# Linear attention gated by an FFN: rest stacks in buffers of their own and at other steps, bias copies at other steps, a rest matmul at four places

## The chip, the cores and the metric

One core of a Trainium2 chip runs the whole kernel. The metric is the device time of one execution in microseconds (us). Several executions are timed and the median is given. One execution is recorded by the hardware profiler; all times inside the kernel are from it, counted from the first instruction.

The core has five engines. TensorE multiplies matrices (PE; PEld is its load of the stationary operand), VectorE (DVE), ScalarE (ACT) and GpSimd (POOL) work on tiles in the on-chip memory, and SyncE (SP) issues most DMA transfers. Each engine works through its own instructions in order.

## What is computed

```python
def reference(x, wqkv, wo, w1, b1, w2, b2):          # x: 1 x 2048 x 576, F = 4608
    xn = layernorm(x)
    q, k, v = split(xn @ wqkv)                       # 32 heads of 18
    pq, pk = phi(q), phi(k)                          # phi(t) = where(t > 0, t + 1, exp(t)) + 1e-6
    kv, z = einsum(pk, v), sum(pk)                   # one state per head, no softmax
    s = (pq @ kv / (pq @ z + 1e-6)) @ wo
    g = silu(gelu(xn @ w1 + b1) @ w2 + b2)
    return x + s * g
```

Everything is float32. There are two halves, a linear attention and an FFN of width 4608, and the FFN's silu gates the attention's output.

## The kernel before

Every product is computed from a high and a low part of each operand: a cast on ScalarE makes the high part (hi), a subtraction on VectorE the low part (lo), and three matmuls (high by high, high by low, low by high) stand for one. The large products are also split into blocks and computed with seven block products in place of eight, which needs sums of blocks of both operands, made once and kept in DRAM where they are used more than once.

The program has three stages.

*Pairs 0 to 7* (to 155 us). A pair is two row tiles of 128 tokens. They are normalized and transposed, keys and values are computed, and the attention state is summed up. In the gaps the block sums of w2 are made (`w2_hi`, `w2_lo`, lines 565 to 577) and stored.

*Pairs 8 to 15 and a last half* (155 to 308 us). Queries are computed, wo is folded into the state, and the attention's output is written per row tile to s_dram. The denominators are made by `den_mul` on GpSimd (line 926).

*The FFN* (308 to 1082 us, then a tail). Tokens are taken in two halves, and for each half F in nine chunks (18 in all, `HOps`). A chunk has two block pairs (`Up`, numbered by `self.p`); for each, `Up.mm` (line 1280 on) makes the seven block products of x by w1 in PSUM, ScalarE applies the gelu, and the down products `pm` (line 1430) are added up in the tile `macc` by VectorE. `macc` starts from the bias b2: `load_bias` (line 1262) brings two rows of it by DMA into two blocks of `macc`, and four calls of `set_bias` (line 1267) copy them on ScalarE to all places. At the half switch the old `macc` is combined and stored to `c_dram` first.

D is 576, that is four blocks of 128 and a rest of 64. The rest's rows (of x and of w1) are handled by `Rest` (line 314): for each of seven stacks it loads a tile of 128 x 512 (`rs`), casts it (`hi`, line 326, ScalarE) and subtracts (`lo`, line 330, VectorE) in two groups of 3 and 4 blocks, `sums` in between (lines 347 and 349, four small instructions), and stores the results (line 341) to `we_dram` or `xe_dram` with SyncE. In the FFN each product has seven matmuls, six for the blocks and one for the rest: `we` by `x_extra` or a piece of x.

What sets the order. The work around the pairs is listed in `plans`, a table from a step number to calls. A pair has 14 steps (`NSP`), step = pair x 14 + position, and at each step the calls filed under it are issued. For the rest stacks `REST_PLAN` (line 792) gives (pair, position) of the load, the first group's lo, the sums and the second group's lo; hi comes a step before lo and the store a step after. A chunk of the FFN has 28 steps (`NS`) in the same table. VectorE, ScalarE, GpSimd and TensorE follow the program's order. SyncE issues its transfers in an order of its own, one after the other, and each waits until an earlier one, mostly the one eight before it, has landed. The stacks' tiles `re` have the tag "stw" of the pool `w1r`, two buffers, which `w2_hi` and other stagings use as well.

Of the kernel before, what the change touches and what calls it, by code (L numbers as in the profile page):

```python
# [9 lines left out]
F32R = mybir.dt.float32r  # L10
# [5 lines left out]
P = 128  # L16
# [23 lines left out]
NSP = 14  # L40
# [5 lines left out]
def linear_attention_gated_ffn(ctx, tc, x, wqkv, wo, w1, w1e, b1, w2, b2, out):  # L46
    nc = tc.nc
# [267 lines left out]
    class Rest:  # L315
# [6 lines left out]
        def hi(self, g):  # L322
            n = (3, 4)[g]
            t = w1r.tile([P, 2, 4, P], F32R, tag="stw", name=f"re{self.i}{self.of_x}{g}")
            self.t[g] = t = t[:, :, :n]
            nc.scalar.copy(t[:, 0], self.s[:, :n])
# [348 lines left out]
    def k_sum(k):  # L675
# [5 lines left out]
    W2_SPLITS = (  # L681
        (2, 4, 6), (2, 9, 12), (3, 4, 6), (3, 9, 12), (4, 4, 6), (4, 9, 12), (5, 7, 9), (6, 7, 9), (7, 1, 3),
    )
# [3 lines left out]
    def plan_pair(p):  # L687
# [102 lines left out]

    rests = {}
    REST_PLAN = {
        (0, True): ((2, 12), (3, 2), (3, 4, GP), (4, 2)),
        (0, False): ((4, 0), (5, 2), (5, 13, DV), (6, 2)),
        (1, False): ((4, 7), (5, 2), (5, 13, DV), (6, 2)),
        (2, False): ((8, 9), (9, 12), (9, 12, DV), (10, 6)),
        (3, False): ((9, 9), (10, 6), (10, 11, DV), (11, 6)),
        (4, False): ((11, 1), (12, 6), (12, 9, DV), (13, 6)),
        (1, True): ((13, 1), (14, 6), (14, 9, DV), (15, 6)),
    }  # L800

    def plan_rests():
        for key, (load, first, (p, k, eng), second) in REST_PLAN.items():
            add(load[0] * NSP + load[1], lambda key=key: rests.update({key: Rest(*key)}))
            for g, (q, at) in enumerate((first, second)):
                step = q * NSP + at
                add(step - 1, lambda key=key, g=g: rests[key].hi(g))
                add(step, lambda key=key, g=g: rests[key].lo(g))
                add(step + (2 if step == 9 * NSP + 12 else 1), lambda key=key, g=g: rests[key].store(g))
            add(p * NSP + k, lambda key=key, eng=eng: rests[key].sums(eng))  # L810

# [57 lines left out]
    kwp = ph2.enter_context(tc.tile_pool(name="kwp", bufs=1, reuse_waits="tile"))  # L869
    t2 = ph2.enter_context(tc.tile_pool(name="t2", bufs=2, side="right", reuse_waits="tile"))  # L870
    wo_sb = []
    for i, (g, n) in enumerate(GROUPS):
# [234 lines left out]
    EL1 = nc.vector  # L1107
    kept = []
    w1t, w2_raw0 = {}, []

# [150 lines left out]

    def load_bias():
        for h, m in enumerate(BIAS):
            src = bass.AP(tensor=b2.tensor, offset=b2.offset + h * HD, ap=[[0, P], [1, HD]])
            nc.sync.dma_start(macc[:, 0, m, :], src)

# [6 lines left out]
    class Up:  # L1273
# [10 lines left out]
        def mm(self, ps, i, first=True):  # L1284
            (wh, wl), (h, l) = self.w.product(i), self.xb[i]
            seq = []
            for k in range(2):
                seq += [(wh[:, k], h[:, k]), (wh[:, k], l[:, k]), (wl[:, k], h[:, k])]
            seq += [(self.w.rest(i), xrest[i])]
            for n, (st, mv) in enumerate(seq):  # L1290
                nc.tensor.matmul(  # L1291
                    ps.rearrange("p (c j) -> p c j", c=4), st, mv, start=first and n == 0, stop=n == len(seq) - 1,
                    skip_group_check=True,
                )
# [329 lines left out]
    n_chunks = 2 * NC  # L1624
    load_bias()
    for step in range(n_chunks):
# [4 lines left out]
        if c == 0:  # L1631
            if half:
                add(base + 8, load_bias)
            for at, m in zip((12, 13, 15, 17), (C11, C22, C21, C12)):
                add(base + at, set_bias, m)
# [148 lines left out]
```

## Time and profile before

| what | us |
|---|---|
| three runs, median (lowest to highest) | 1141.03 (1137.71 to 1145.02) |
| the profiled execution, its time | 1137.64 |
| the profiled execution, its span from first to last instruction | 1135.9 |
| TensorE busy in the span | 1102.8 (97%) |
| mean clock granted to TensorE | 0.986 of full speed |
| VectorE, ScalarE, GpSimd busy | 826.5, 515.7, 452.5 |

The timeline of an engine lists its instructions with the start, the duration, the line, the output and inputs, and in brackets how long the engine was idle before it and who ended that ("<-DVE k L422": VectorE's instruction of line 422 that writes k). Instructions on an engine overlap a little, so a duration can reach into the next start. The windows view gives for a stretch A:B its length, then the busy time and count of instructions on each engine, then the granted TensorE clock, the DMA engines' busy share and GB/s. In the chain of waits each row is a start, a duration and what the end of the kernel hung on then; "DMA a<-b" is the time from a transfer's issue to its landing.

### The profile page before, as it was taken

The page shows a single profiled execution, that of the slowest core. Times are in us where ns is not written, and L with a number is a line of the kernel's source. Part 1 is how long each engine was busy: PE and PEld are TensorE (multiplying, and loading weights), DVE is VectorE, ACT ScalarE, POOL GpSimd, SP SyncE. Part 2 cuts the span into 40 slices and gives each one's busy share as a digit, 9 for nine tenths or more (in the row PEclk, how much of TensorE's full clock was granted, in tenths as well). Part 3 has the DMA queues.
Part 4 walks back from the last instruction along what each step waited for, and adds up shares of the span by engine and source line. Part 5 has one row for each costly group of instructions (what it writes and reads, how often), then busy time and mean ns, then how long its engine had stood idle before and what let it go on. Part 6 is the DMA issues. An engine that isn't in the chain of part 4 may idle for free.

```text
span 1135.9 us, 18977 instructions
## 1 busy us (share of the span) xinstructions
PE 1102.8 (97%) x6888; PEld 1018.9 (90%) x6888; DVE 826.5 (73%) x1284; ACT 515.7 (45%) x945; POOL 452.5 (40%) x421
## 2 busy tenths in 40 slices
PE   8999998999999999999999999979999999999998
PEld 8999997999989989989889899878998988989988
DVE  6776857888588878888888788655674664755766
ACT  7765645554564444554544444433242242342342
POOL 6844153454552543544534524313232242341310
PEclk9999898999999999999999999989999999999999
DMA  5989856896998796796887969987667667777343
GB/s 203 322 281 346 306 177 195 293 349 229 331 376 292 249 358 202 274 341 215 309 293 231 349 195 358 386 310 254 201 231 232 217 219 226 220 223 230 96 147 119
DMA packets 116059, 295.02 MB, mean 260 GB/s; under 512 B 12221, under 2 KB 31677, under 8 KB 113919
## 3 DMA queue, kind: packets, MB, share of 16 engines
q1 hardware_dynamic: 110495, 282.61, 70.3%
q0 software_dynamic: 4896, 10.03, 5.4%
q8 instruction: 54, 0.88, 0.3%
q10 hardware_dynamic: 576, 1.18, 0.3%
q14 instruction: 38, 0.31, 0.1%
HBM read 180.39 MB, written 108.66 MB: 254 GB/s over the span
## 4 chain that ended last, share of the span: by engine, by line
PE 79%; DMA 7%; DVE 6%; ACT 3%; issue 3%; POOL 1%; SPq 1%; DVEq 0%; POOLq 0%; ACTq 0%
PE pm L1430 33%; PE zy L1291 10%; PE a L1291 9%; PE e L1291 9%; PE b L1291 5%; PE ps_s L989 4%; PE pd L1545 2%; PE e L414 1%; PE pl L470 1%; PE z L414 1%; DMA wa<-op_a 1%; DMA rs2False<-w1e 1%; PE a L414 1%; DMA op<-w2o 1%; DMA op<-w 1%
## 5 line engine op out<-in xcount | busy, mean ns | idle before, releaser
L1019 ACT CAST h_h<-g 128x512 fp32r<-128x512 f32 x204 | 120.2, 621 | 137.8 <-PE pm L1430 136.6
L1022 DVE TENSOR_TENSOR h_l<-g,h_h 128x512 fp32r<-128x512 f32 x204 | 161.5, 792 | 8.9 <-ACT h_h L1019 8.9
L1438 DVE TENSOR_TENSOR macc<-macc,pm 128x576 f32<-128x576 f32 x136 | 102.1, 751 | 40.1 <-PE pm L1430 40.1
L1291 PE MATMUL a<-xH,wa 128*128 128x512 f32 x288 | 101.4, 393 | 0.0
L1440 DVE TENSOR_TENSOR macc<-pm,macc 128x576 f32<-128x576 f32 x98 | 74.2, 757 | 24.9 <-PE pm L1430 23.5
L1398 POOL TENSOR_TENSOR mid<-g 128x512 f32<-128x512 f32 x34 | 44.5, 1309 | 105.2 <-ACT g L1299 105.2
L1299 ACT ACTIVATE g<-b,b1c 128x512 f32<-128x512 f32 x36 | 24.8, 688 | 134.6 <-DVE b L1317 134.6
L1291 PEld LDWEIGHTS a<-xH,wa 128*128 128x128 f32 x288 | 54.0, 188 | 11.3
L1308 ACT COPY mid<-a 128x512 f32<-128x512 f32 x36 | 21.2, 588 | 94.7 <-PE a L1291 94.7
L1392 POOL TENSOR_TENSOR g<-g 128x512 f32<-128x512 f32 x34 | 49.9, 1468 | 25.8 <-DVE h_l L1022 24.4
L1311 DVE TENSOR_TENSOR mid<-b,mid 128x512 f32<-128x512 f32 x36 | 24.7, 685 | 44.8 <-PE b L1291 42.8
L1395 POOL TENSOR_TENSOR g<-g 128x512 f32<-128x512 f32 x34 | 51.3, 1508 | 12.5 <-DVE h_l L1022 10.4
L1291 PE MATMUL a<-xL,wa 128*128 128x512 f32 x144 | 56.2, 390 | 0.0
L1516 POOL TENSOR_TENSOR fin1l<-fin1h,fin1l 128x288 f32<-128x288 f32 x8 | 6.5, 807 | 120.4 <-DVE macc L1438 42.6
L1291 PE MATMUL e<-xSH,wb 128*128 128x512 f32 x144 | 50.5, 391 | 1.3 <-DVE b L1317 1.1
L1291 PE MATMUL zy<-xSH,w 128*128 128x512 f32 x144 | 50.9, 394 | 0.0
L1291 PE MATMUL zy<-xH,w 128*128 128x512 f32 x144 | 50.9, 394 | 0.0
L1291 PE MATMUL b<-xSH,w 128*128 128x512 f32 x144 | 50.5, 391 | 0.0
L1291 PE MATMUL e<-xSH,w 128*128 128x512 f32 x144 | 50.4, 390 | 0.0
L1389 POOL TENSOR_TENSOR g<-g 128x512 f32<-128x512 f32 x34 | 47.1, 1385 | 2.7
L1046 POOL TENSOR_TENSOR mid<-w1raw 128x256 f32<-128x256 f32 x17 | 13.3, 782 | 84.7 <-DMA w1raw<-w 57.3
L676 POOL TENSOR_TENSOR zacc<-zacc,k 128x576 f32<-128x576 f32 x16 | 25.6, 1602 | 53.2 <-ACT k L507 52.6
(965 smaller groups left out, 3711.3 us busy)
## 6 DMA issues: line engine op xcount, KB each, us to landing
op<-w SPq DMA_DIRECT2D x72, 256.0 KB
w<-op SPq DMA_DIRECT2D x72, 256.0 KB
we<-we_dram SPq DMA_DIRECT2D x36, 448.0 KB
w2raw<-w SPq DMA_DIRECT2D x10, 1152.0 KB
op<-w2o SPq DMA_DIRECT2D x19, 576.0 KB
w1raw<-w SPq DMA_DIRECT2D x18, 512.0 KB
op_a<-wa SPq DMA_DIRECT2D x18, 512.0 KB
wa<-op_a SPq DMA_DIRECT2D x18, 512.0 KB
```

Source lines behind the costliest of these rows:

```text
L414: nc.tensor.matmul(ps, st, mv, start=first and n == 0, stop=n == len(seq) - 1, skip_group_check=True,)
L989: nc.tensor.matmul(self.ps[h], st[:, k, :], w[:, k, h * HD : (h + 1) * HD], start=(i == 0), stop=(i == len(self.seq) - 1),)
L1019: nc.scalar.copy(pair[0], src)
L1022: eng.tensor_tensor(pair[1], src, pair[0].bitcast(F32), op=SUB)
L1291: nc.tensor.matmul(ps.rearrange("p (c j) -> p c j", c=4), st, mv, start=first and n == 0, stop=n == len(seq) - 1, skip_group_check=True,)
L1389: tt(src[5, pr], A(1, 1), A(1, 0), op=SUB)
L1392: tt(src[6, pr], src[5, pr], A(0, 0), op=ADD)
L1395: tt(src[3, pr], src[6, pr], A(0, 1), op=SUB)
L1398: tt(src[7, pr], A(0, 0), A(1, 0), op=SUB)
L1430: nc.tensor.matmul(ps[:, q, :HD], hs[p][st][:, cs], m[:, p, :], start=(n == 0 and i not in CHAIN), stop=(n == len(seq) - 1), skip_group_ch ...
L1438: nc.vector.tensor_tensor(dst, dst, src, op=SUB)
L1440: nc.vector.tensor_tensor(dst, src, dst, op=ADD)
```

## The change

It has four parts.

*Rest stacks.* The tiles `re` get a pool and tag of their own: in the pairs the pool `t1` with one buffer, from pair 8 on the pool `t2` with two. `REST_PLAN` has new steps for loads, groups and sums; at most one of the early stacks is in work in a pair. Stack (2, False) is loaded in the set-up of the second stage. The sums of five stacks stand at position 6 or earlier of a pair (two of them behind position 9 to 13 before). The sums of (0, True) stay on GpSimd, a pair later; the others stay on VectorE. The split of w2's sum 6 in pair 5 moves three positions earlier.

*Half 0's bias.* Its load is unchanged; the four copies move from steps 12, 13, 15 and 17 of the first chunk to 5, 6, 7 and 8, the second and third in swapped order.

*Half 1's bias.* Its load moves from step 8 of the chunk on SyncE's queue to step 5 on GpSimd's; the copies move to steps 10, 11, 13 and 14.

*The rest matmul.* In `Up.mm` it was the last of the seven of a product. It is now the seventh, first, fourth or sixth for block pairs 0, 1, 2 and 3 (by `self.p % 4`).

```diff
--- before.py
+++ after.py
@@ -321,7 +321,8 @@
 
         def hi(self, g):
             n = (3, 4)[g]
-            t = w1r.tile([P, 2, 4, P], F32R, tag="stw", name=f"re{self.i}{self.of_x}{g}")
+            pool, bufs = rest_pool
+            t = pool.tile([P, 2, 4, P], F32R, tag="re", name=f"re{self.i}{self.of_x}{g}", bufs=bufs)
             self.t[g] = t = t[:, :, :n]
             nc.scalar.copy(t[:, 0], self.s[:, :n])
 
@@ -679,7 +680,7 @@
 
     K_UP = (1, 6, 7, 5, 2, 4, 3)
     W2_SPLITS = (
-        (2, 4, 6), (2, 9, 12), (3, 4, 6), (3, 9, 12), (4, 4, 6), (4, 9, 12), (5, 7, 9), (6, 7, 9), (7, 1, 3),
+        (2, 4, 6), (2, 9, 12), (3, 4, 6), (3, 9, 12), (4, 4, 6), (4, 9, 12), (5, 4, 6), (6, 7, 9), (7, 1, 3),
     )
     W2_STARTS = ((1, 7), (2, 2), (2, 11), (3, 2), (3, 11), (4, 2), (4, 11), (6, 0), (6, 8))
     W2_LOADS = {1: (13, 1), 3: (7, 2), 5: (7, 3)}
@@ -788,26 +789,30 @@
         if p == 6:
             add(base + 12, lambda: wkq.sums(cur["rq"][0], GP))
 
-    rests = {}
+    rests, rest_pool = {}, (t1, 1)
     REST_PLAN = {
-        (0, True): ((2, 12), (3, 2), (3, 4, GP), (4, 2)),
-        (0, False): ((4, 0), (5, 2), (5, 13, DV), (6, 2)),
-        (1, False): ((4, 7), (5, 2), (5, 13, DV), (6, 2)),
-        (2, False): ((8, 9), (9, 12), (9, 12, DV), (10, 6)),
-        (3, False): ((9, 9), (10, 6), (10, 11, DV), (11, 6)),
-        (4, False): ((11, 1), (12, 6), (12, 9, DV), (13, 6)),
-        (1, True): ((13, 1), (14, 6), (14, 9, DV), (15, 6)),
+        (0, True): ((3, 0), (4, 2), (4, 4), (5, 2)),
+        (0, False): ((4, 7), (5, 13), (6, 2), (6, 4)),
+        (1, False): ((5, 7), (6, 12), (6, 13), (7, 4)),
+        (2, False): (None, (9, 12), (10, 6), (10, 11)),
+        (3, False): ((10, 12), (11, 6), (12, 6), (13, 6)),
+        (4, False): ((12, 12), (13, 6), (14, 6), (15, 6)),
+        (1, True): ((14, 12), (15, 6), (16, 1), (16, 3)),
     }
 
+    def load_rows(key):
+        rests[key] = Rest(*key)
+
     def plan_rests():
-        for key, (load, first, (p, k, eng), second) in REST_PLAN.items():
-            add(load[0] * NSP + load[1], lambda key=key: rests.update({key: Rest(*key)}))
+        for key, (load, first, sums, second) in REST_PLAN.items():
+            if load:
+                add(load[0] * NSP + load[1], load_rows, key)
             for g, (q, at) in enumerate((first, second)):
                 step = q * NSP + at
                 add(step - 1, lambda key=key, g=g: rests[key].hi(g))
                 add(step, lambda key=key, g=g: rests[key].lo(g))
-                add(step + (2 if step == 9 * NSP + 12 else 1), lambda key=key, g=g: rests[key].store(g))
-            add(p * NSP + k, lambda key=key, eng=eng: rests[key].sums(eng))
+                add(step + {9 * NSP + 12: 2, 16 * NSP + 3: 0}.get(step, 1), lambda key=key, g=g: rests[key].store(g))
+            add(sums[0] * NSP + sums[1], lambda key=key, eng=GP if sums[0] == 4 else DV: rests[key].sums(eng))
 
     plan_rests()
     for p in range(1, NPAIR):
@@ -868,6 +873,7 @@
     ph2 = ExitStack()
     kwp = ph2.enter_context(tc.tile_pool(name="kwp", bufs=1, reuse_waits="tile"))
     t2 = ph2.enter_context(tc.tile_pool(name="t2", bufs=2, side="right", reuse_waits="tile"))
+    rest_pool = (t2, 2)
     wo_sb = []
     for i, (g, n) in enumerate(GROUPS):
         wo_sb.append(stage(D, f"wo{i}"))
@@ -1106,6 +1112,7 @@
     EW1 = nc.gpsimd
     EL1 = nc.vector
     kept = []
+    load_rows((2, False))
     w1t, w2_raw0 = {}, []
 
     def den_all(r, s):
@@ -1259,10 +1266,10 @@
 
     BIAS = (C11, C22)
 
-    def load_bias():
+    def load_bias(eng):
         for h, m in enumerate(BIAS):
             src = bass.AP(tensor=b2.tensor, offset=b2.offset + h * HD, ap=[[0, P], [1, HD]])
-            nc.sync.dma_start(macc[:, 0, m, :], src)
+            eng.dma_start(macc[:, 0, m, :], src)
 
     def set_bias(s):
         m = BIAS[s in (C12, C22)]
@@ -1286,7 +1293,7 @@
             seq = []
             for k in range(2):
                 seq += [(wh[:, k], h[:, k]), (wh[:, k], l[:, k]), (wl[:, k], h[:, k])]
-            seq += [(self.w.rest(i), xrest[i])]
+            seq.insert((6, 0, 3, 5)[self.p % 4], (self.w.rest(i), xrest[i]))
             for n, (st, mv) in enumerate(seq):
                 nc.tensor.matmul(
                     ps.rearrange("p (c j) -> p c j", c=4), st, mv, start=first and n == 0, stop=n == len(seq) - 1,
@@ -1622,7 +1629,7 @@
     seq = ExitStack()
     seq.enter_context(in_order(nc.vector.engine, nc.scalar.engine, nc.gpsimd.engine, nc.tensor.engine))
     n_chunks = 2 * NC
-    load_bias()
+    load_bias(nc.sync)
     for step in range(n_chunks):
         half, c = divmod(step, NC)
         base = step * NS
@@ -1630,8 +1637,8 @@
         h = HOps(c)
         if c == 0:
             if half:
-                add(base + 8, load_bias)
-            for at, m in zip((12, 13, 15, 17), (C11, C22, C21, C12)):
+                add(base + 5, load_bias, nc.gpsimd)
+            for at, m in zip((10, 11, 13, 14) if half else (5, 6, 7, 8), (C11, C21, C22, C12)):
                 add(base + at, set_bias, m)
         if half == 0:
             plan_w1(add, w1t[2 * step + 1], base, **P1)
```

How the instructions are moved shows at three places. The first is ScalarE in pair 6, where `xn` is the normalized tile, `xH` and the tiles behind it are copies of the transposed x, and `k_170<-a` makes keys from the PSUM tile that the next value products take over. Before:

```order
L477 COPY v_167<-pl_1624 128x288
L303 COPY scr<-pt_1588 128x640
L426 COPY mu_161<-a_1680 128x288
L279 ACTIVATE xn_1691<-x_1319,mv_1614 128x576
L279 ACTIVATE xn_1691<-x_1319,mv_1614 128x64
L326 CAST re0False_1702<-rs0False 128x512
L326 CAST re1False_1704<-rs1False 128x512
L299 CAST xH<-pt_1738 128x384
L300 CAST x_tmp1h<-pt_1738 128x256
L354 COPY xr_1746<-pt_1738 64x128
L438 ACTIVATE k_170<-a_1680,c_84 128x288
```

and now:

```order
L478 COPY v_167<-pl_1614 128x288
L303 COPY scr<-pt_1581 128x640
L427 COPY mu_161<-a_1665 128x288
L279 ACTIVATE xn_1678<-x_1312,mv_1604 128x576
L279 ACTIVATE xn_1678<-x_1312,mv_1604 128x64
L327 CAST re0False_1709<-rs0False 128x512
L299 CAST xH<-pt_1721 128x384
L300 CAST x_tmp1h<-pt_1721 128x256
L355 COPY xr_1729<-pt_1721 64x128
L439 ACTIVATE k_170<-a_1665,c_84 128x288
L502 ACTIVATE e_168<-k_170,c_85 128x576
L379 CAST xSH<-scr 128x1152
```

The cast of re1False left this pair, and re0False's second group stands where it stood; it now uses the buffer of the first group, whose stores SyncE issues behind the loads of wqkv in this pair.

The second place is ScalarE in the first chunk of the FFN, with the gelus of the first block pair, the casts `w_0` of w2's blocks and the bias copies (`macc<-macc`; they stood a block pair later). Before:

```order
L1299 ACTIVATE g<-e_3747,b1c 128x512
L1299 ACTIVATE g<-zy_3746,b1c 128x512
L1308 COPY mid<-a_3871 128x512
L1019 CAST h_h<-g 128x512
L1019 CAST w_0__3897<-w2raw_3498 128x576
L1019 CAST w_0__3911<-w2raw_3498 128x576
L1019 CAST h_h<-g 128x512
L1299 ACTIVATE g<-b_3872,b1c 128x512
```

and now:

```order
L1306 ACTIVATE g<-e_3747,b1c 128x512
L1278 COPY macc<-macc 128x3x288
L1306 ACTIVATE g<-zy_3746,b1c 128x512
L1278 COPY macc<-macc 128x4x288
L1315 COPY mid<-a_3873 128x512
L1278 COPY macc<-macc 128x3x288
L1025 CAST h_h<-g 128x512
L1278 COPY macc<-macc 128x4x288
L1025 CAST w_0__3901<-w2raw_3489 128x576
L1025 CAST w_0__3915<-w2raw_3489 128x576
L1025 CAST h_h<-g 128x512
```

All four bias copies now stand ahead of the two casts of w2 and the second `h_h`.

The third place is GpSimd at the half switch, where line 1453 combines the first half's blocks in `macc` and line 1405 is the next chunk's first sum. Now:

```order
L1402 TENSOR_TENSOR g<-g 128x512
L1453 TENSOR_TENSOR macc<-macc 128x2x288 x2
L1272 DMA macc<-b 128x288 x2
L1405 TENSOR_TENSOR mid<-g 128x512
L1396 TENSOR_TENSOR g<-g 128x512
L1399 TENSOR_TENSOR g<-g 128x512
L1402 TENSOR_TENSOR g<-g 128x512
```

Before, no DMA stood on GpSimd here; the two loads stood on SyncE behind the weights of the second chunk.

## Prediction

> **What bounds the kernel now.** I read the page first, then the chain of waits, then TensorE's timeline for its idle gaps, then the timeline of the engine that each gap names. Columns: start, duration, engine, line, output<-inputs, and in brackets the idle time before it and what ended it.
>
> ```profile
> PE 1102.8 (97%) x6888; PEld 1018.9 (90%) x6888; DVE 826.5 (73%) x1284; ACT 515.7 (45%) x945; POOL 452.5 (40%) x421
> 355.43 1.62 PE a L1291 x7
> ...
> 400.38 1.62 PE a L1291 x7
> ...
> 736.76 6.34 DMA macc<-b
> 355.00:400.00 45.00, 45.00 (x269) 40.76 (x268) 37.72 (x56) 22.26 (x44) 20.43 (x19) 1.00 0.81 278
> ```
>
> TensorE is busy 97% of the span. In the FFN a chunk is TensorE's work alone: between 355 and 400 us it is busy 45.00 of 45.00 us at a granted clock (third number from the end) of 1.00, and two chunks' first products (chain rows of 355.43 and 400.38) start 44.95 us apart. Nothing there can be won without removing matmuls, and the change removes none. What can move is the 33 us in which TensorE stands still, and the time after each stop in which its clock is low. The gaps of over a microsecond behind the points that the diff touches:
>
> ```profile
> 75.38 0.40 PE L414 MATMUL e<-wkq_h,xSH 128*128 128x288 f32 x1 [2.44 <-DVE k L422]
> 114.83 0.61 PE L414 MATMUL e<-wkq_h,xSH 128*128 128x288 f32 x1 [3.19 <-DVE k L422]
> 191.22 0.40 PE L414 MATMUL a<-wkq_h,xH 128*128 128x288 f32 x1 [3.11 <-ACT scr L426]
> 193.75 0.61 PE L414 MATMUL z<-wkq_h,xH 128*128 128x288 f32 x1 [1.16 <-DVE scr L432]
> 239.59 0.80 PE L956 MATMUL ptp<-ident,pbuf 128*128 128x128 f32 x5 [1.91 <-DVE th L968]
> 273.60 0.73 PE L956 MATMUL ptp<-ident,pbuf 128*128 128x128 f32 x5 [1.91 <-DVE th L968]
> 75.00:78.00 3.00, 2.62 (x14) 2.63 (x15) 2.92 (x9) 2.22 (x6) 1.34 (x3) 0.72 1.04 360
> 78.00:81.00 3.00, 3.00 (x19) 3.00 (x19) 2.38 (x6) 2.50 (x3) 0.00 (x0) 0.71 0.69 233
> 114.00:117.00 3.00, 2.17 (x9) 2.18 (x10) 2.92 (x9) 2.10 (x6) 0.00 (x0) 0.50 0.84 301
> 117.00:120.00 3.00, 3.00 (x14) 3.00 (x14) 2.03 (x5) 2.30 (x3) 0.00 (x0) 0.50 0.83 261
> 193.00:196.00 3.00, 2.25 (x9) 2.25 (x10) 2.85 (x7) 1.48 (x3) 1.03 (x1) 0.50 0.98 317
> 196.00:199.00 3.00, 3.00 (x15) 3.00 (x14) 2.90 (x7) 0.00 (x0) 1.14 (x1) 0.50 1.05 425
> 239.00:242.00 3.00, 2.41 (x13) 2.44 (x14) 1.86 (x4) 0.87 (x4) 0.00 (x0) 0.69 0.39 153
> 242.00:245.00 3.00, 3.00 (x19) 3.00 (x18) 1.58 (x4) 0.86 (x2) 0.00 (x0) 0.74 0.96 305
> ```
>
> Each gap costs its idle time and, for about 6 us behind it, the work that the lower clock does not do: busy time times one minus the clock. So the gap at 75 costs 2.44 + 0.28 x 2.62 + 0.29 x 3.00 = 4.1 us; the one at 115 costs 3.19 + 0.50 x 2.17 + 0.50 x 3.00 and a little behind it = 6.0; the pair at 191 and 194 costs 4.27 + 0.50 x 2.25 + 0.50 x 3.00 = 6.9; the one at 240 costs 1.91 + 0.31 x 2.41 + 0.26 x 3.00 = 3.4, and I take the same for 274.
>
> **The change part by part.** The rows that name the causes:
>
> ```profile
> 73.85 0.51 ACT L326 CAST re0True<-rs0True 128x384 fp32r<-128x384 f32 x1 [6.51 <-issue]
> 113.30 0.51 ACT L326 CAST re1False<-rs1False 128x384 fp32r<-128x384 f32 x1 [6.67 <-issue]
> 190.36 0.51 ACT L326 CAST re2False<-rs2False 128x384 fp32r<-128x384 f32 x1 [2.81 <-DMA rs2False<-w1e]
> 180.09 10.25 DMA rs2False<-w1e
> 235.07 3.46 DVE L349 TENSOR_TENSOR rs4False<-rs4False 128x128 f32<-128x128 f32 x4
> 191.50 1.27 DVE L349 TENSOR_TENSOR rs2False<-rs2False 128x128 f32<-128x128 f32 x4
> 230.88 3.66 POOL L562 TENSOR_TENSOR w2r<-w2r 128x576 f32<-128x576 f32 x2
> ```
>
> ScalarE runs in order, and in the first three rows it stands at the cast of a rest stack with its next copies queued behind; those feed VectorE's k or the scr copy for which TensorE waits. At 73.85 the stack's load is late: now it is asked for fifteen steps ahead of its cast instead of three. At 113.30 it is a buffer of the tag that it shares with the w2 stores: now it has a pool of its own and one stack per pair. At 190.36 it is the load that took 10.25 us: now it is queued right behind wo's, more than a pair earlier. In all three the next thing to be late is VectorE's ordinary work, which kept TensorE fed in the neighbouring pairs. I take all of it: 4.1 + 6.0 + 6.9 = 17.0 us.
>
> At 235 the four sums take 3.46 us where the same four took 1.27 at 191.50; GpSimd's w2 sum of 230.88 runs up to the start of it and its den products follow. The transposes' copy th is behind them. Now the sums stand at step 6 of the pair, ahead of that stretch. in pairs 12 and 14, where that step had a group's lo; in pairs 13 and 15 two groups' lo come together there, some 1.1 us of VectorE against the 0.6 of one. Between nothing and 6.8 us back; nearest to the row of 1.27 us, so 5.5. The sums that stay GpSimd's (re0True) come a pair later, and the w2 split of pair 5 three steps earlier: the same instructions on engines that had idle time at both places, taken at nothing; were that cover gone, it would be a split's 0.7 us of ScalarE (the row of 322.65 below has such a cast).
>
> The half switch:
>
> ```profile
> 743.12 0.91 ACT L1271 COPY macc<-macc 128x864 f32<-128x864 f32 x1 [5.81 <-DMA macc<-b]
> 746.00 0.85 PE L1430 MATMUL pm<-w__8258,h_h 128*128 128x288 f32 x2 [5.73 <-DVE macc L1442]
> 746.00:749.00 3.00, 3.00 (x12) 3.00 (x13) 1.46 (x2) 3.00 (x4) 2.84 (x3) 0.50 1.06 396
> 749.00:752.00 3.00, 3.00 (x15) 3.00 (x14) 2.17 (x2) 0.74 (x3) 1.82 (x2) 0.50 0.55 219
> 713.86 3.92 POOL L1446 TENSOR_TENSOR macc<-macc 128x576 f32<-128x576 f32 x2 [14.05 <-DVE macc L1438]
> 716.42 0.60 SPq L1505 DMA_DIRECT2D c_dram<-macc  x1
> ```
>
> The bias is asked for at 736.76 on SyncE's queue and lands at 743.10; ScalarE waits 5.81 us for it, TensorE 5.73, and 3.0 us go to the clock: 8.7. Now it is asked for on GpSimd's queue right behind the sum of 713.86. It must still wait until the old values are stored; the first store is issued at 716.42, and with the same 6.34 us from issue to landing the first load starts near 723 to 725 and is there by 732, ScalarE's first copy being due at 733.6. GpSimd's sum behind the second load, due at 727.45, is held to about 731 to 732, and its reader has a step of slack. 8.0 of 8.7 us come back; the bounds are 0 (late all the same) and 8.7.
>
> **What it costs.** Three places, all where a wait is added in front of queued work.
>
> First, pair 6. All early stacks now use one buffer. ScalarE's cast of the second group of re0False waits until the first group's stores have landed.
>
> ```profile
> 132.02 0.67 SPq L596 DMA_DIRECT2D rr<-wqkv  x1
> 132.78 1.08 SPq L341 DMA_DIRECT2D we_dram<-re0False  x2
> 133.46 6.95 DMA we_dram<-re0False
> 133.90 0.50 ACT L438 ACTIVATE k<-a,c 128x288 f32<-128x288 f32 x1 [0.16 <-PE a L414]
> ```
>
> On SyncE's queue these stores stand behind five loads of wqkv, so they are issued at 132.78 and, by the row below, land at 138 to 140.4. ScalarE would reach the cast at 131.5, and queued behind it are the x copies and the k of 133.90, which TensorE needs at 135.8. k comes 4 to 7 us late, TensorE stands for 3 to 5.5 us, and the clock costs up to 3 more. Bounds 0 (the stores overtake the loads) and 9; I take 7, since the landing is from a row of this very store. In pair 7 the second group of re1False stands the same way in front of the k copy, behind shorter stores: 0 to 2.5, I take 1.
>
> Second, chunk 0. The four bias copies move from behind 332 us, where they stand among the next pair's gelus, to a place ahead of w2's casts:
>
> ```profile
> 322.65 0.68 ACT L1019 CAST w__3897<-w2raw 128x576 fp32r<-128x576 f32 x1
> 328.19 0.68 DVE L1317 TENSOR_TENSOR b<-e,mid 128x512 f32<-128x512 f32 x1
> 328.93 0.50 PE L1291 MATMUL e<-xSH,wb 128*128 128x512 f32 x1 [1.13 <-DVE b L1317]
> ```
>
> Two of 0.8 and two of 1.05 us (the row of 743.12, less its overlap) put 3.7 us ahead of the cast at 322.65. VectorE, in order too, stands at that cast's lo; the add of 328.19, for which TensorE already waits 1.13 us, comes 1.7 to 3.3 us later. At 2.8 us and more of idleness the clock falls as in the rows above. Bounds 0 and 6; I take 4.
>
> Third, the load of x_extra (1 MB) now stands behind w1's loads and the last rest stores, ahead of we's, near 300 us instead of 287.40. The same bytes are ahead of we as before, in another order, so it costs only the queue's idle moments: 0 to 4, I take 1.
>
> The rest matmul's place in a product costs nothing: each of the seven matmuls has its own weight load already (6888 of each on the page), and a product of seven takes 1.62 us, by the chain's row of 355.43.
>
> **The sum.** 17.0 + 5.5 + 8.0 = 30.5 back, 7 + 1 + 4 + 1 = 13 lost: 17.5. The profiled execution took 1137.64 us (span 1135.9), so 1120 on its footing. It lies 3.4 under the median of the three runs, 1141.03, at their lower end of 1137.71; I put 2 us of that on: **1122 us**, 1112 to 1130 by the terms' own bounds.
>
> [...]
>
> **The rivals.**
>
> 1. *The bias is late from GpSimd's queue too.* The second load waits for a later store, and GpSimd is held behind it. For it: the wait of 5.81 us is a whole DMA latency, and a late first copy brings the gap back. Against it: 8 us of margin or more on the first store. Without those 8 us: 1130. [...]
>
> 2. *The added waits are hidden.* Stores land before the casts are due, and chunk 0 absorbs the copies. For it: half as many bytes are stored in that pair as before, and in chunk 0 ScalarE stood idle 4.48 us ahead of 328.91. Against it: the 6.95 us row, and VectorE's order in chunk 0. Of the 13 lost some 11 come back: 1111.
>
> 3. *The waits cost more than thought.* The cast in pair 6 holds VectorE's and the transposes' work of pair 7 too, TensorE stands twice, and chunk 0 loses its 6 us: 9 more than forecast, 1131, within the noise.
>
> 4. *Slower: the rest matmul's new place breaks the overlap of weight loads.* There are 252 such matmuls (36 block pairs of seven products) and 182 move (26 pairs).
>
> ```profile
> L1291 PEld LDWEIGHTS a<-xSH,we x2: 187/188/188, 309.5 to 320.7; 128*128 128x128 f32 x2
> ```
>
> If each move exposed one load of 188 ns, 182 of them cost 34.2 us: 1122 + 34.2 = 1156. It decides from about 105 ns each (19 us over 182). Against it: 1.62 us over seven are 231 ns for each, at every change of weights, so a load hides behind the matmul ahead wherever it stands.
>
> **How the numbers follow.** Forecast 0.50, rival 1 0.12, rival 2 0.17, rival 3 0.14, rival 4 0.07. One per cent is 11.4 us, about what a measurement of this kernel can tell from no change, so faster means under 1129.6. The forecast nearly whole (0.47) and rival 2 give 0.64, and a part of rival 1 0.04: faster 0.68. Slower is rival 4 and a little of rival 3: 0.08. Within 1%: 0.24. The range, 1109 to 1138, takes in rivals 1 to 3 and leaves out the slower one.
>
> **What would show it.** Right: no TensorE gap over 1 us near 75, 115 and 191; the sums of rs4False near 1.3 us; ScalarE not waiting for macc<-b, and a first chunk of half 1 of 45 to 46 us; a new ScalarE wait of 5 to 8 us at the second re0False cast; a larger gap than 1.13 us at chunk 0's e. Chunks in between as long as before. Wrong: chunks at another length (rival 4), the gap at the half switch still there (rival 1), or old gaps that only changed what they wait for.

## The result and the profile after

The changed kernel takes 1130.75 us (median of 7 runs, 1126.47 to 1133.49), the kernel before 1141.03 (7 runs, 1137.71 to 1145.02). The ratio is 0.9908, 95% interval 0.988 to 0.9936: 10.3 us less. Forecast were 19 less, 1122, with a range of 1109 to 1138. The profiled execution of the changed kernel is the slowest of its seven, 1133.49 us with a span of 1131.4; that of before was among its fastest, with 1135.9. So the two profiles differ by 4.5 us of span, and they have to be accounted for by that number.

All of TensorE's gaps that the prediction listed are gone, the one at the half switch too; of the pair at 191 and 194 us 0.81 us is left (at 194.78). These are the gaps over a microsecond behind 50 us in the changed kernel (timeline of TensorE; in brackets the idle time and what ended it):

```profile
135.26 0.61 PE L471 MATMUL pl<-wv_h,xH 128*128 128x288 f32 x1 [8.39 <-ACT k L439]
155.92 0.40 PE L471 MATMUL pl<-wv_h,xH 128*128 128x288 f32 x1 [2.15 <-ACT k L439]
288.72 0.77 PE L962 MATMUL ptp<-ident,pbuf 128*128 128x128 f32 x5 [1.22 <-POOL pbuf L945]
307.15 0.76 PE L1298 MATMUL a<-xSH,we 128*128 128x512 f32 x1 [6.18 <-DMA we<-we_dram]
330.70 0.50 PE L1298 MATMUL e<-x_extra,we 128*128 128x512 f32 x1 [3.77 <-DVE b L1324]
```

Four of the five stand where the prediction had put a new wait: pair 6, pair 7, the FFN's start and the first chunk's e. The windows behind them (length, busy time and count by engine, then granted clock, DMA share, GB/s) give the rest of their price:

```profile
135.00:138.00 3.00, 2.74 (x11) 2.74 (x12) 2.92 (x10) 0.37 (x2) 0.00 (x0) 0.50 0.52 186
138.00:141.00 3.00, 3.00 (x18) 3.00 (x17) 1.80 (x4) 3.00 (x5) 0.00 (x0) 0.67 0.47 175
156.00:159.00 3.00, 3.00 (x16) 3.00 (x17) 2.29 (x4) 1.15 (x2) 0.00 (x0) 0.68 0.89 329
159.00:162.00 3.00, 3.00 (x19) 3.00 (x19) 1.47 (x2) 3.00 (x5) 0.00 (x0) 0.76 0.89 255
306.00:309.00 3.00, 1.85 (x5) 1.49 (x6) 0.00 (x0) 1.05 (x3) 0.00 (x0) 0.50 1.00 385
309.00:312.00 3.00, 3.00 (x11) 2.42 (x10) 1.71 (x3) 1.79 (x4) 1.56 (x2) 0.72 0.50 135
330.00:333.00 3.00, 2.30 (x6) 1.87 (x7) 2.63 (x4) 2.29 (x4) 2.10 (x2) 0.69 1.00 358
333.00:336.00 3.00, 3.00 (x12) 2.41 (x11) 1.48 (x3) 1.42 (x3) 1.60 (x2) 0.74 1.04 406
```

By the prediction's own rule (idle time, and busy time times one minus the clock) pair 6 costs 8.39 + 1.37 + 0.99 = 10.8 us, pair 7 2.15 + 0.96 + 0.72 = 3.8, the FFN's start 6.18 + 0.93 + 0.84 = 8.0, and the first chunk 3.77 + 0.71 + 0.78 = 5.3, of which 1.1 was there before. With the 1.22 us at 288.72, 28 us are lost. The gaps that are gone were worth 4.1 + 6.0 + 6.9 + 6.8 + 8.7 = 32.5. The difference, some 4.5 us, is that of the two spans. The medians of the seven runs differ by 10.3, so between usual executions the balance is some 6 us better than between these two; which of the terms differ is not shown.

The causes are named by ScalarE's timeline, for the FFN's start by SyncE's and the chain of waits, and for the first chunk by VectorE's:

```profile
133.39 0.62 ACT L327 CAST re0False<-rs0False 128x512 fp32r<-128x512 f32 x1 [13.30 <-DMA we_dram<-re0False]
...
154.85 0.62 ACT L327 CAST re1False<-rs1False 128x512 fp32r<-128x512 f32 x1 [2.63 <-DMA we_dram<-re1False]
```

```profile
286.01 1.76 SPq L1036 DMA_DIRECT2D w1raw<-w  x2
287.87 0.81 SPq L870 DMA_DIRECT2D w2raw<-w  x1
288.74 1.43 SPq L342 DMA_DIRECT2D xe_dram<-re1True  x2
292.11 0.53 SPq L1248 DMA_DIRECT2D x_extra<-xe_dram  x1
293.36 3.11 SPq L1081 DMA_DIRECT2D we<-we_dram  x2
```

```profile
293.36 13.65 DMA we<-we_dram
```

```profile
327.41 0.76 DVE L1028 TENSOR_TENSOR w__3901<-w2raw,w__3901 128x576 fp32r<-128x576 f32 x1 [2.26 <-ACT w__3901 L1025]
```

ScalarE stands for 13.30 us at the second cast of re0False, for the first group's store. At the FFN's start the load of we takes 13.65 us from issue to landing, behind everything above it, which was issued in the seven microseconds ahead of it. In the first chunk VectorE stands 2.26 us for a cast of w2 that the bias copies hold up. DMA share is the number before the last in the windows; in the changed kernel it is full from 276 us on (0.96 to 1.03), where in the kernel before the same 8 us were less than half used (the third line; from 284 us on the share is 0.84 to 0.96 there too):

```profile
276.00:284.00 8.00, 8.00 (x64) 8.00 (x63) 7.45 (x9) 5.43 (x11) 5.40 (x4) 1.00 0.99 315
300.00:308.00 8.00, 1.82 (x7) 1.25 (x6) 0.76 (x2) 0.95 (x4) 0.78 (x2) 0.74 1.03 389
```

```profile
276.00:284.00 8.00, 8.00 (x56) 8.00 (x56) 6.44 (x14) 2.56 (x7) 2.90 (x3) 0.89 0.43 168
```

At the half switch the changed kernel's GpSimd waits twice for the old values' stores, and the sum behind the second load starts at 736.52; ScalarE's first bias copy no longer waits, and TensorE is busy 44.42 of the 45 us, its largest gap there 0.29 us (at 740.68):

```profile
727.03 0.61 POOL L1272 DMA_DIRECT2D macc<-b  x1 [6.33 <-DMA c_dram<-macc]
735.94 0.57 POOL L1272 DMA_DIRECT2D macc<-b  x1 [8.30 <-DMA c_dram<-macc]
736.52 1.30 POOL L1405 TENSOR_TENSOR mid<-g 128x512 f32<-128x512 f32 x1
```

```profile
715.00:760.00 45.00, 44.42 (x260) 39.85 (x259) 31.52 (x42) 22.56 (x32) 16.96 (x12) 1.00 1.03 383
```

### The profile page after: what moved, and what is told of

Read it like the earlier page. It is cut to its first block, busy times and chain, and to the rows that moved or that the text cites. A ratio compares the mean times of both kernels' runs of the same rounds, so it can differ in the third digit from the quotient of the medians.

```text
span 1131.4 us, 18969 instructions
## 1 busy us (share of the span) xinstructions
PE 1097.3 (97%) x6888; PEld 1013.0 (90%) x6888; DVE 820.2 (72%) x1284; ACT 516.5 (46%) x945; POOL 455.3 (40%) x423
## 4 chain that ended last, share of the span: by engine, by line
PE 84%; DMA 7%; DVE 3%; ACT 2%; issue 1%; SPq 1%; POOL 1%; DVEq 0%; ACTq 0%; POOLq 0%
PE pm L1437 34%; PE zy L1298 9%; PE e L1298 9%; PE a L1298 9%; PE b L1298 5%; PE pl L471 5%; PE ps_s L995 3%; PE e L415 2%; PE pd L1552 2%; PE a L415 2%; PE z L415 2%; DMA we<-we_dram 1%; DMA c_dram<-macc 1%; PE ps_kva L524 1%; DMA w2r<-w 1%
## 5 line engine op out<-in xcount | busy, mean ns | idle before, releaser
L1298 PEld LDWEIGHTS a<-xH,wa 128*128 128x128 f32 x288 | 54.0, 188 | 11.4
L1298 PE MATMUL b<-xSH,w 128*128 128x512 f32 x144 | 52.9, 399 | 0.0
```

The lines of the kernel that those rows point to most:

```text
L1298: nc.tensor.matmul(ps.rearrange("p (c j) -> p c j", c=4), st, mv, start=first and n == 0, stop=n == len(seq) - 1, skip_group_check=True,)
```

## The experiments

Eleven kernels, each timed in five rounds beside the kernel before. Ratios are to the kernel before, whose median was 1139.6 to 1139.9 in these runs; the changed kernel's is 0.9908 (0.988 to 0.9936).

| run | median, us | ratio (95%) |
|---|---|---|
| e1 early stacks spread | 1125.9 | 0.9884 (0.9862 to 0.9905) |
| e2 x_extra early | 1125.66 | 0.9874 (0.9855 to 0.9894) |
| e3 first chunk's old bias steps | 1126.36 | 0.9885 (0.9863 to 0.9908) |
| e4 rest matmul last | 1129.9 | 0.992 (0.9899 to 0.9941) |
| e5 second buffer | 1117.94 | 0.9814 (0.9788 to 0.9839) |
| e6 kernel before, half 1's bias alone | 1130.77 | 0.9912 (0.9895 to 0.9929) |
| e7 two sums late | 1127.56 | 0.9902 (0.9878 to 0.9926) |
| e8 e5 + e2 + e3 | 1114.93 | 0.9774 (0.9755 to 0.9793) |
| e9 late stacks at their old steps | 1134.24 | 0.995 (0.9932 to 0.9967) |
| e10 e5 + e3 | 1115.63 | 0.9784 (0.9766 to 0.9803) |
| e11 e10, last stack's stores early, we ahead of x_extra | 1110.12 | 0.9738 (0.972 to 0.9757) |

**Pairs 6 and 7.** First the same single buffer with the casts spread out:

```diff
-        (0, True): ((3, 0), (4, 2), (4, 4), (5, 2)),
-        (0, False): ((4, 7), (5, 13), (6, 2), (6, 4)),
-        (1, False): ((5, 7), (6, 12), (6, 13), (7, 4)),
+        (0, True): ((3, 0), (4, 2), (4, 4), (4, 11)),
+        (0, False): ((4, 7), (5, 5), (5, 6), (5, 13)),
+        (1, False): ((5, 7), (6, 8), (6, 9), (7, 4)),
```

> The changed kernel with the three early rest stacks' groups spread so that the single buffer is free again when the next cast comes: (0, True) second group at (4, 11), (0, False) at (5, 5) and (5, 13), (1, False) at (6, 8) and (7, 4). Theory (the one buffer's stores are what ScalarE waits for in pairs 6 and 7): the gaps of 8.39 and 2.15 us at the value products go, with the clock lost behind them about 10.8 + 3.8 = 14.6 us, so 11 to 15 us less than the changed kernel's 1130.75, near 1117. Rival (the time won is only waited for later, because the transfers ahead of the FFN already fill the DMA engines): the gap of 6.18 us at we grows by as much as is won, and the time stays within 4 us of 1130.75.

The two gaps went, and others of 2.56, 2.73 and 2.04 us came at 113.67, 140.13 and 143.50. ScalarE's timeline shows why: it waits for the buffer's store at the new places.

```profile
109.88 0.51 ACT L327 CAST re0False<-rs0False 128x384 fp32r<-128x384 f32 x1 [3.01 <-DMA xe_dram<-re0True]
...
136.31 0.51 ACT L327 CAST re1False<-rs1False 128x384 fp32r<-128x384 f32 x1 [4.81 <-DMA we_dram<-re0False]
```

Only 3 us by the ratio and 5 by the median came back, not 11 to 15. The gap at we did not grow (3.43 us), so the rival's reason was not the cause either. The next run therefore left the plan nearly alone and gave a second buffer to the second group of (0, False); the first group of (1, False) moved two positions up besides:

```diff
-            pool, bufs = rest_pool
-            t = pool.tile([P, 2, 4, P], F32R, tag="re", name=f"re{self.i}{self.of_x}{g}", bufs=bufs)
+            pool, tag, bufs = (w1r, "stw", 2) if g and rest_pool[0] is t1 and (self.of_x, self.i) == (False, 0) else (rest_pool[0], "re", rest_pool[1])
+            t = pool.tile([P, 2, 4, P], F32R, tag=tag, name=f"re{self.i}{self.of_x}{g}", bufs=bufs)
...
-        (1, False): ((5, 7), (6, 12), (6, 13), (7, 4)),
+        (1, False): ((5, 7), (6, 10), (6, 12), (7, 4)),
```

> The changed kernel with the plan as changed, but the second group of stack (0, False) takes one of the two buffers it used before the change (tag stw), and the first group of (1, False) stands two positions earlier in pair 6, ahead of the next pair's x stores. Theory (it is one buffer held by a store, not where the casts stand, that stops ScalarE): the gap of 8.39 us goes and that of 2.15 falls below 1, 11 to 14 us less than the changed kernel, 1117 to 1120. Rival (a cast of a stack stops something wherever it stands, as the spread plan did): new gaps of 2 to 3 us, 4 to 6 us less, as in the spread plan.

The ratio fell by 0.0094, 10.7 us, at the lower end of the theory; no gap over 0.9 us is left before 276 us. The same cast now waits for the sums of its own stack alone, 1.99 us, with nobody late behind it:

```profile
121.88 0.62 ACT L327 CAST re0False<-rs0False 128x512 fp32r<-128x512 f32 x1 [1.99 <-DVE rs0False L350]
```

What stopped ScalarE in pair 6 is the one buffer, held by a store for some 7 us. The wait in pair 7 went as well; whether by the second buffer or by the moved group was not told apart.

**The FFN's start.** The last stack's place decides where SyncE's order has x_extra:

```diff
-        (1, True): ((14, 12), (15, 6), (16, 1), (16, 3)),
+        (1, True): ((13, 12), (14, 12), (15, 6), (15, 12)),
```

> The changed kernel with the last stack, (1, True), at ((13, 12), (14, 12), (15, 6), (15, 12)): SyncE's order then has the x_extra load ahead of w1's loads as before the change, and the stack's last stores behind the FFN's first weights. Theory (2 MB more stand ahead of we in the queue): the gap of 6.18 us at we goes, 6 to 8 us less than 1130.75. Rival (we is late because its own issue waits for w1raw and w2raw, whatever is ahead): the gap stays at 4 us or more and the time moves by under 3 us.

The gap at we is gone and 5 us of the median (4 by the ratio) came back, not 6 to 8: the gap at the first chunk's e grew from 3.77 to 4.76 us, since a cast of w2 there now waits 2.08 us for the last stack's store, and one of 1.60 us came at the half switch. So theory it is, with part of the gain given back later.

**The first chunk's bias.**

```diff
-            for at, m in zip((10, 11, 13, 14) if half else (5, 6, 7, 8), (C11, C21, C22, C12)):
+            for at, m in zip((10, 11, 13, 14) if half else (12, 15, 13, 17), (C11, C21, C22, C12)):
```

> The changed kernel with the first chunk's four bias copies back at steps 12, 13, 15 and 17; half 1's stay as changed. Theory (the copies hold up w2's casts, and VectorE's order the rest): the gap of 3.77 us at the first chunk's e falls to 1.2 us or less, and 3 to 4.5 us come back. Rival (the gap is there because the first chunk starts late and its weights with it): gap and time stay within 1 us.

The gap at e fell to 1.59 us, not quite the 1.2 that was expected, but close to the 1.13 of before:

```profile
323.83 0.50 PE L1298 MATMUL e<-x_extra,we 128*128 128x512 f32 x1 [1.59 <-DVE b L1324]
```

The time went down by 2.6 us on the ratio and 4.4 on the median. The intervals of this run and of the changed kernel overlap, and the gap at we is smaller too in this run's profile (2.46 us against 6.18), which the bias copies cannot be given the credit for. So the gap at e is shown, and its worth in time is not.

**The rest matmul's place.**

```diff
-            seq.insert((6, 0, 3, 5)[self.p % 4], (self.w.rest(i), xrest[i]))
+            seq += [(self.w.rest(i), xrest[i])]
```

> The changed kernel with the rest matmul last in every product, as before. Theory (each matmul has its own weight load, hidden behind the one ahead): chunks stay at 44.9 us and the time within 2 us of 1130.75. Rival (first, fourth or sixth exposes or hides a load): chunks of another length, from 0.2 us a chunk on, 4 us or more in all.

The time is the same within its interval. In the chain of waits the first products of two chunks start 44.89 us apart with the matmul last (first fence) and at the four places (second, the changed kernel), and each takes 1.62 us:

```profile
354.90 1.62 PE a L1298 x7
...
399.79 1.62 PE a L1298 x7
```

```profile
358.17 1.62 PE a L1298 x7
...
403.06 1.62 PE a L1298 x7
```

**The half switch alone**, in the kernel before:

```diff
-            for at, m in zip((12, 13, 15, 17), (C11, C22, C21, C12)):
+            for at, m in zip((10, 13, 11, 14) if half else (12, 13, 15, 17), (C11, C22, C21, C12)):
...
-                add(base + 8, load_bias)
+                add(base + 5, load_bias, nc.gpsimd)
```

> The kernel before with one part of the change alone: half 1's bias load on GpSimd's queue and its four copies at the new steps. Theory (the gap of 5.73 us at the half switch is the bias's DMA latency alone): the gap goes and 7 to 9 us come back, 1132 against 1140. Rival (GpSimd's queue is held until the old values are stored, and the copies come late again): a gap of 2 us or more stays there and under 4 us come back.

Ratio 0.9912, 10.0 us (9.1 between the medians); no gap over 0.6 us is left behind 305 us. This one part is worth about as much as the whole change.

**The sums beside GpSimd.** In the changed kernel the gaps near 240 and 274 are gone, but the sums are not shorter:

```profile
228.35 4.14 DVE L350 TENSOR_TENSOR rs3False<-rs3False 128x128 f32<-128x128 f32 x4
```

So either their place or something else took the gaps away. Two stacks' sums back late:

```diff
-        (3, False): ((10, 12), (11, 6), (12, 6), (13, 6)),
-        (4, False): ((12, 12), (13, 6), (14, 6), (15, 6)),
+        (3, False): ((10, 12), (11, 6), (12, 9), (13, 6)),
+        (4, False): ((12, 12), (13, 6), (14, 9), (15, 6)),
```

> The changed kernel with two of the sums back late in their pair: stack (3, False) at (12, 9) and (4, False) at (14, 9). Theory (what stops TensorE is the transposes' copy queued behind the sums, so the place decides and not how long they take): gaps of 1.5 to 2 us at the transposes near 230 and 263 us come back, 5 to 7 us more than 1130.75. Rival (the dilation beside GpSimd decides): they are as long at position 6, so the move changes nothing, within 2 us.

The time did not change, and only small gaps came back, 0.47 and 0.51 us where 1.5 to 2 were expected: the place alone does not decide. Nor are the sums as long as the rival took them to be, since here they take 2.37 us, not 4.14 as at position 6. They start behind a step (line 505) for which VectorE waits 1.63 us:

```profile
228.21 1.02 DVE L505 SCALAR_TENSOR_TENSOR rt<-e,rt 128x576 f32<-128x576 f32 x1 [1.63 <-ACT e L502]
...
231.04 2.37 DVE L350 TENSOR_TENSOR rs3False<-rs3False 128x128 f32<-128x128 f32 x4
```

```profile
234.47 0.74 PE L962 MATMUL ptp<-ident,pbuf 128*128 128x128 f32 x5 [0.47 <-DVE th L974]
```

What the kernel before had and this one has not is a group's lo in the same pair. So all four late stacks went back to their old steps:

```diff
-        (2, False): (None, (9, 12), (10, 6), (10, 11)),
-        (3, False): ((10, 12), (11, 6), (12, 6), (13, 6)),
-        (4, False): ((12, 12), (13, 6), (14, 6), (15, 6)),
-        (1, True): ((14, 12), (15, 6), (16, 1), (16, 3)),
+        (2, False): (None, (9, 12), (9, 12), (10, 6)),
+        (3, False): ((9, 9), (10, 6), (10, 11), (11, 6)),
+        (4, False): ((11, 1), (12, 6), (12, 9), (13, 6)),
+        (1, True): ((13, 1), (14, 6), (14, 9), (15, 6)),
```

> The changed kernel with the four late stacks' groups and sums at the steps of before (the load of (2, False) stays early, the buffers as changed); SyncE's order then has x_extra ahead of w1's loads again. Theory (a stack's lo and its sums in one pair, both drawn out beside GpSimd, were too much for the transposes' copy): the two gaps of 1.9 us near 230 and 265 come back (7 us), the gap of 6.18 at we goes (8 us): 1128 to 1132. Rival (the buffers and the load made those gaps, not the steps): they stay away, and with the one at we gone the time is near 1123.

Both gaps are back, and the one at we is gone (VectorE's and TensorE's timelines):

```profile
230.47 1.14 DVE L331 TENSOR_TENSOR re4False<-rs4False,re4False 128x384 fp32r<-128x384 f32 x1
232.19 1.33 DVE L505 SCALAR_TENSOR_TENSOR rt<-e,rt 128x576 f32<-128x576 f32 x1 [0.58 <-ACT e L502]
...
235.34 3.47 DVE L350 TENSOR_TENSOR rs4False<-rs4False 128x128 f32<-128x128 f32 x4
```

```profile
239.87 0.73 PE L962 MATMUL ptp<-ident,pbuf 128*128 128x128 f32 x5 [1.90 <-DVE th L974]
...
272.31 0.74 PE L962 MATMUL ptp<-ident,pbuf 128*128 128x128 f32 x5 [1.89 <-DVE th L974]
```

So the steps made the two gaps, not the buffers or the early load. Within the pair the lo (first row) falls into time in which VectorE was idle in the run before: the step of line 505 still waits for ScalarE's e, 0.58 us in place of 1.63. From there on the two runs differ by 0.3 us up to the sums and by 1.10 in the sums, 3.47 against 2.37 us, and the gap by 1.43. So it is how long the sums take at this late place that sets the gap, as far as two traces tell; it was not changed by itself. A lo and the sums of one stack also stand together in pair 10 of this run (at 202.69, and 3.63 us of sums at 206.33) without a gap at the transposes, so sharing a pair is not enough. The median is 2 us over the expected range. A gap of 3.21 us at 195.18 that no theory had may be why; a lo and the sums of (2, False) stand at one step there, which was not tried by itself.

**All waits out at once.** First the three of e5, e2 and e3 together:

> The changed kernel with the second buffer, x_extra early and the first chunk's old bias steps together. Theory (the three waits are independent): 11 to 14, 5 and 4 us come back, 20 to 23 in all, 1108 to 1111. Rival (what is won ahead of the FFN is waited for there, since the DMA engines are full from 276 us on): a gap at the FFN's start takes 4 us or more of it, 1115 or more.

The rival was right in the outcome: a gap of 5.31 us stands at the first chunk's e, where ScalarE waits at a cast of w2. By the row it is not w2 that is late there (a cast from the same tile ran at 296.24 already) but the last stack's store, issued at 299.79; in e10, with that store out at 275.06, this wait is gone. Why the cast needs the store the trace does not say:

```profile
308.74 0.67 ACT L1025 CAST w__3893<-w2raw 128x576 fp32r<-128x576 f32 x1 [6.35 <-DMA xe_dram<-re1True]
```

Then without e2, to tell whose gap that is:

> The changed kernel with the second buffer and the first chunk's old bias steps; the late stacks as changed, so x_extra and 1 MB of stores stand ahead of we. Theory (the gap of 5.31 us in the three-fix kernel is the late stores' doing, which hold up w2's last block): the gap at the first chunk's e is 1.6 us or less, that at we 2.5 to 4, and the time 1113 to 1116. Rival (w2's block is late because TensorE comes earlier): a gap of 4 us or more at e here too, 1117 or more.

At e 0.77 us are left, so the late stores made that gap; instead the one at we is 4.19:

```profile
291.72 0.76 PE L1298 MATMUL a<-xSH,we 128*128 128x512 f32 x1 [4.19 <-DMA we<-we_dram]
```

Both orders cost the same, 1115 to 1116 us. The last run sends the stores ahead of w1's loads and we ahead of x_extra:

```diff
-        (1, True): ((14, 12), (15, 6), (16, 1), (16, 3)),
+        (1, True): ((13, 8), (14, 8), (15, 6), (15, 9)),
...
-    load_x_extra(0)
     for n in range(2):
         w1t[n].load_rest()
+    load_x_extra(0)
```

> As the last, and (1, True) at ((13, 8), (14, 8), (15, 6), (15, 9)), so that its last stores go out ahead of w1's loads, and we's loads stand ahead of x_extra's. Theory (order in the queue decides what is late at the FFN's start): the gap at we goes or falls below 2 us, 3 to 5 us less than the last kernel, near 1110. Rival (the DMA engines are full there, so another transfer is late by as much): a gap of 3 us or more moves to x_extra's product or the first chunk's e, and the time stays within 2 us.

1110.12 us, ratio 0.9738 (0.972 to 0.9757): 30 us under the kernel before and 19 under the changed one, by the ratios. The largest gap at the FFN's start is that of x_extra's product:

```profile
290.65 0.50 PE L1298 MATMUL b<-x_extra,we 128*128 128x512 f32 x1 [0.97 <-DMA x_extra<-xe_dram]
```

The DMA engines are as full there as before (share 1.00 and 1.03 from 276 to 292 us); what is needed last now stands last. Two transfers moved at once here; which of them brings the 5 us was not told apart.

## Why the prediction was right, and where its sum was wrong

The sign and the places were right, and so were the mechanisms but for the transposes' and for the timing of two waits. Of 19 us forecast 10.3 came. By the prediction's own line (faster means under 1129.6) 1130.75 is "within 1%", to which it gave 0.24, and not "faster", to which it gave 0.68. The range held because it was wide: 1130.75 lies just outside the 1112 to 1130 given as the terms' own bounds. (Those bounds, added up term by term, give 1107 to 1144.) Between the two profiles 17.5 us were forecast and 4.5 came.

*The gains.* 30.5 us were forecast and 32.5 came: all of the gaps at 75, 115, 191 and 194 (but for the 0.8 us left there), of both transposes, and of the half switch, which e6 shows alone with 9 to 10 us. For the transposes the step that failed was "nearest to the row of 1.27 us": the sums did not become shorter, they take 4.14 us where 1.3 was written down as the sign. In their new place they do no harm even so; late in the pair their length decides, as far as e7 and e9 tell: 0.47 us of gap with 2.37 us of sums, 1.90 with 3.47.

*Pair 6 and pair 7: mis-sized, 8 forecast, 14.6 measured*, both above their bounds of 9 and 2.5 us. The store of re0False, issued at 126.42, held ScalarE until 133.39, nearly the 6.95 us of the row of before. (That row is the second group's store there, not "this very store"; in the changed kernel it is the first group's.) The step that failed was "ScalarE would reach the cast at 131.5". On the clock of before it is there at 129.21, and the same sum had just taken 10.1 us out ahead of it: ScalarE came at 120.1 (133.39 less 13.30), 11.4 us sooner than written down. The store came at 126.42 instead of 132.78, only 6.4 us sooner. By the chain of waits its second half waited until the store of xr, issued at 119.80, had landed, 7.22 us later:

```profile
129.21 0.64 ACT L326 CAST re0False<-rs0False 128x512 fp32r<-128x512 f32 x1
```

```profile
119.80 7.22 DMA xr_dram<-scr
...
127.08 6.21 DMA we_dram<-re0False
```

The waiting engine gained more than what it waits for. Nor does the new plan leave "one stack per pair": by `REST_PLAN`, pairs 5 and 6 each hold groups of two early stacks.

*The FFN's start: mis-sized, 1 forecast, 8.0 measured.* The step that failed was "the same bytes are ahead of we as before, in another order, so it costs only the queue's idle moments". Before, x_extra was asked for at 287.40 and the last stack's stores at 282.52, ten and fifteen microseconds ahead of w1's loads at 297.55; now these 4 MB are issued together, in the seven microseconds ahead of we, and e2, which puts x_extra ahead again and the last stores behind, has no gap there. TensorE also came earlier, at 300.97 (307.15 less 6.18) instead of the 309.73 of before, but that does not show as a cause: in e5 it came at 288.31, sooner still, and waited 2.51 us. This wait is also what varies: over runs with the same order of transfers there it was 6.18, 5.52, 4.19, 3.74, 3.43, 2.51 and 2.46 us (the changed kernel, e4, e10, e7, e1, e5, e3).

*The first chunk: 4 forecast, 4.1 measured*, by the way that was named, and e3 takes the gap back to 1.59 us. *The rest matmul: nothing*, as e4 shows. *GpSimd at the switch:* its sum was forecast for 731 to 732 and came at 736.52, of which 2.9 us are the later start of this part (716.78 against 713.86). Here it costs TensorE 0.29 us, but 0.56, 0.93, 1.31 and 1.60 in e6, e5, e10 and e2, each time for ScalarE's cast that waits for this sum; "its reader has a step of slack" is only just so.

Of the rivals, the third (the waits cost more than thought) comes nearest: it gave 1131. Its reasons are not those of the runs: TensorE does stand twice, but the second time for a store of pair 7's own, the first chunk cost what was forecast, and the FFN's start is not in it. That the number agrees is luck.

How much of the changed kernel's spread comes from the wait at we stays open; it was not tried by itself. The mean granted clock of its seven executions runs from 0.989 to 0.993, and 0.004 of 1130 us is 4.5 us, by estimate, of the 7 us between the slowest and the fastest.

## What to carry to other kernels

When several stalls are taken out of one chain, redo the arrival times on both sides of each new wait before sizing it: in pair 6 the waiting engine came 11.4 us sooner than written down and the store it waits for 6.4, while at the FFN's start the transfers moved up with TensorE (in e5 it was there at 288.31 and waited 2.51 us). In pair 6 the store issued at 126.42 kept its buffer until 133.39, half of it behind the store of xr; with a second buffer (e5) the wait of 13.30 us at that cast fell to 1.99, while the casts spread out over the one buffer (e1) waited 3.01 and 4.81 us. So count a second buffer before spreading the work out. Where DMA is full (share 1.00 and 1.03 in e11 from 276 to 292 us), ask of each transfer when it is needed and put the last needed last: the same bytes in three orders (e8, e10, e11) cost 1115, 1116 and 1110 us.

## What the runs showed of the hardware

Two things were not expected. The prediction charges every gap that it lists with a lower clock behind it, and writes "At 2.8 us and more of idleness the clock falls". In these runs it did not always fall. In all thirteen traces, between 60 and 350 us and around the half switch, there are 28 gaps of 1.60 to 3.43 us; behind 19 of them the clock was lower in the next 3 us, and behind 9 it stayed at 1.00. The first line is the window of the 1.90 us gap at 239.87 of e9, with the clock at 1.00 where the same gap of the kernel before (1.91 us) has 0.69. Then come a gap of 3.36 us without a fall (e6, unchanged there from the kernel before, which has 0.50) and one of 1.60 us with it (e2):

```profile
239.00:242.00 3.00, 2.13 (x17) 2.16 (x18) 2.14 (x4) 0.55 (x2) 0.00 (x0) 1.00 0.37 149
```

```profile
115.24 0.40 PE L414 MATMUL e<-wkq_h,xSH 128*128 128x288 f32 x1 [3.36 <-DVE k L422]
115.00:118.00 3.00, 2.76 (x20) 2.76 (x21) 2.92 (x10) 1.52 (x4) 0.00 (x0) 1.00 0.92 295
```

```profile
734.34 0.54 PE L1437 MATMUL pm<-w__8226,h_h 128*128 128x288 f32 x2 [1.60 <-ACT h_h L1025]
737.00:740.00 3.00, 3.00 (x17) 3.00 (x16) 0.96 (x2) 2.51 (x4) 2.84 (x3) 0.62 1.02 412
```

All 17 gaps of 3.5 us and more in these stretches had a fall (to 0.50 and 0.69 in the windows behind the 6.18 and 3.77 us of the changed kernel). Behind gaps under 1.6 us the clock stayed at 1.00, as behind 288.72 of the changed kernel (1.22 us, the line below), but for two that stand close behind a gap of over 3 us. So the 28 gaps cost their idle time, and the 19 up to nearly as much again, by the prediction's estimate (6.0 us in all for the gap of 3.19); these runs do not show what decides it. A reading by which such gaps cost their idle time alone fits the 9 and not the 19. The clock may be part of what tells one execution from the next (its mean was 0.989 to 0.993 in the changed kernel's seven).

```profile
291.00:294.00 3.00, 2.96 (x24) 2.75 (x23) 0.93 (x2) 1.47 (x4) 1.76 (x2) 1.00 1.03 430
```

And four subtractions of 128 x 128 on VectorE took 1.27 us at 191.50 of the kernel before, 2.37 at 231.04 of e7, 3.46 at 235.07 of the kernel before and 4.14 at 228.35 of the changed kernel. In these four rows, the longer they took, the more of their time GpSimd had an instruction running: 0.25, 1.7, 3.0 and 3.6 us. That GpSimd makes them longer was not tried by itself, and beside its issue of a transfer (0.94 us at 121.01 of the changed kernel) four of them took 1.26 us. The sums of rs3False took 4.14 us at position 6 of their pair and 2.37 at position 9 (e7): moved by a few steps they had another length, and only the timeline of the new kernel told it.
